# A fixed table of operations and engines in place of a planner, with the shared port handed over both ways

## The chip, the cores and the metric

One core of a Trainium2 chip runs the whole program. It has five engines with a queue each: TensorE (PE) for products, VectorE (DVE), ScalarE (ACT) and GpSimd (POOL) for elementwise work, and SyncE (SP), which here only issues transfers; GpSimd and ScalarE issue transfers too. An instruction waits at the head of its queue for semaphores of other engines, and whatever stands behind it waits with it. The metric is the device time of one execution in microseconds (us), the median of three runs.

## The reference

Attention with a sigmoid in place of the softmax (8 batches, 12 heads, 448 positions of 64 columns), and on its result `x` (8 x 448 x 768) a block with a gate, which is a causal convolution of five taps:

```python
scores = scale * np.matmul(q, k.transpose(0, 1, 3, 2)) - np.log(S)
attn = 1.0 / (1.0 + np.exp(-scores))
x = np.matmul(attn, v)                        # then (B, S, H * D)
for k in range(K):                            # K = 5, xp is x after 4 rows of zeros
    gate_pre += conv_w[k][None, None, :] * xp[:, k:k + S, :]
gate = 1.0 / (1.0 + np.exp(-gate_pre))
val = x @ w_val
return (gate * val @ w_out).astype(np.float32)
```

## The kernel before

**Tiles and stages.** The 96 pairs of batch and head are taken two by two (a pair of heads is 128 partitions), and two such pairs make a "two": 24 of them, three to a batch. For each two PE computes scores (L736, and L780 for the rest of 448 = 3 x 128 + 64), ACT takes the sigmoid (L803) out of the PSUM ring `ps_a` (three buffers), and PE multiplies by `v` (L861, L853). The first nine twos keep the sigmoid in one float32 tile `a_single`. From two 9 on, ACT scales it to an f16 part of `a` (L545 through `scaled`), and DVE makes the remainder (L814); `v` is split likewise into `v_hi` and `v_lo` (L834), and the `qk` of the later pairs into `qk_hi` (a transfer by GpSimd, L711) and `qk_lo` (GpSimd, L550).

The result of a two is copied out of PSUM as `x` (a plain copy for the first twos). Its gate starts with tap 0 as a scaled copy (`gate<-x,cw`); DVE adds taps 1 and 2 (L934), GpSimd makes taps 3 and 4 (`tap`, L931) and adds them by a transfer that accumulates (`gate<-tap`, L938); ACT takes the sigmoid (L940). `x` is split into `xs`, PE makes the val product (L1008), DVE multiplies by the gate (`y`, L1040 and its siblings), `y` is split into `g` and PE makes the out product, for the last three batches in another form (L1100) with `f`, `forms` and `parts`, the last of these added up by L1112 and L1117.

In the first 130 us the weights are made ready besides, six column groups of `w_val` and six of `w_out`: 64-bit words to float32 (`w_words`, of which one step, `rebias`, is a scaled copy), the column's largest value (`val_max`, `out_max`), and a split into `w_val_hi` or `w_out_hi` (`w_hi`) and the remainder (L633).

**What sets the order.** Every operation is recorded with the engines that can do it (`ways`, with a cost in us), a priority and the buffers that it reads and writes. `Plan.issue` then plays the program through as a simulation with those costs: at every time at which an engine is free it takes the ready operation of the least priority. Nearly every priority is overwritten by the tuple `ORDER`, which has one number for each operation. Some scaled copies can go to ACT or DVE (`way`); the simulation sends these to ACT unless ACT is taken for long, but those listed in `ON_VECTOR` go to DVE.

**The shared port.** DVE and GpSimd are taken to share a port, and the simulation lets only one of them run an operation marked `VG` at a time. In the program this becomes a wait in one direction: a GpSimd operation waits for the last DVE operation issued before it. GpSimd's transfers have an empty mark and stand outside of it.

Of the kernel before, what the change touches and what calls it, by code (L numbers as in the profile page):

```python
# [43 lines left out]

# [23 lines left out]

# [3 lines left out]

# [34 lines left out]
AT = dict(  # L107
    first=-4.84, step=186.61, val=-515.91, val_step=75.14, out=-1381.77, out_step=211.97, w_max=499.11,
    w_split=-1182.64, load_qk_first=93.79, load_qk=-2337.48, load_v=1519.38, split_hi=399.85, split_lo=-1153.45,
    rest_first=3068.94, rest=-748.49, a_first=-6991.19, a=-90.43, attend=3226.15, v_max=-214.11, v_exp=-1741.71,  # L110
    v_split=-21.46, x=-2502.94, x_max=-489.67, x_scale=476.16, x_hi=572.53, x_lo=137.58, x_step=3687.57,
    x_early=1650.13, first_max=-343.88, tap=856.2, scores=10.18, a_rest=-547.44, a_rest_first=3711.59,
    tap_first=-337.56, tap_pair=-756.79, tap_step=-337.16, gate=2964.81, product=-1112.59, y=2073.03, g_hi=-1655.49,
    g_lo=-4238.48, o=-5658.32, sums=-1096.57, f=-1122.62, late=-18.26, late_step=570.16, late_load=-455.78,
    pair0=2247.51, pair1=-2185.81, pair2=1410.89, pair3=-3009.11, pair4=1393.75, pair5=-5139.43, pair6=1171.29,
    pair7=-1574.89, pair8=1873.65, pair9=-3931.76, pair10=-780.12, pair11=-656.47, pair12=-3903.55, pair13=-1833.8,
    pair14=1272.88, pair15=-560.26, pair16=527.11, pair17=-4581.08, pair18=-2091.41, pair19=954.34, pair20=113.09,
    pair21=-5387.69, pair22=-2231.28, pair23=643.85, val0=-743.06, val1=1226.04, val2=-946.96, val3=1007.5,
    val4=-4230.95, val5=285.08, out0=79.95, out1=2694.58, out2=3666.47, out3=583.13, out4=2673.53, out5=78.95,
    val_of1=-1932.29, val_of2=-2571.71, val_of3=458.2, val_of4=1531.79, val_of5=1383.92, val_of6=-402.85,  # L120
    val_of7=1447.91, out_of1=621.51, out_of2=-1106.68, out_of3=-2449.73, out_of4=-3262.98, out_of5=101.95,
    out_of6=-338.25, out_of7=-4452.36, share=2435.36, w_load=2254.8,
)
# [1213 lines left out]
```

## Time and profile before

| | us |
|---|---|
| median of 3 runs (lowest to highest) | 573.35 (573.22 to 573.49) |
| span of the profiled execution | 572.0 |
| PE busy | 563.5 |
| DVE busy | 422.3 |
| ACT busy | 403.0 |
| POOL busy | 243.8 |

The span goes from the first to the last recorded instruction of one execution; the median is the device time of other executions of the same program and has 1.35 us around that span. Busy times are for the engine's instructions without semaphore and transfer-issuing ones. A sum for the change is made in the span.

### The profile page before, as it was taken

Reading aid. Unit: us, or ns where it says so; the run is one execution under the profiler, and the core shown is the slowest. Engines: PE = TensorE matmul, PEld = TensorE weight load, DVE = VectorE, ACT = ScalarE, POOL = GpSimd, SP = SyncE. Lnnn points to the kernel's source line nnn. Section 1 sums busy time; section 2 is a strip of 40 time slices with the busy share of each in tenths; the row PEclk is TensorE's granted clock in tenths of the full one; section 3 lists DMA queues with packets and bytes.
Section 4 is the critical chain, followed back from the end, with each engine's and each line's share of the span. In section 5 each row is a group of like instructions: output and inputs, shape, how many; then the busy total and the mean of one; then the engine's idle time right before and its main releaser. Section 6 shows DMA issues by size and latency. Waiting matters only on the chain.

```text
span 572.0 us, 9979 instructions
## 1 busy us (share of the span) xinstructions
PE 563.5 (99%) x3793; PEld 300.7 (53%) x3793; DVE 422.3 (74%) x651; ACT 403.0 (70%) x489; POOL 243.8 (43%) x303
## 2 busy tenths in 40 slices
PE   8999999999999999999999999999999999999996
PEld 4343334354554555545454555455555446865785
DVE  0768899897689784586756788867788999847543
ACT  5788986465987869676686977997889995332221
POOL 0001356755755475356734465544656432500000
PEclk9999999999999999999999999999999999999999
DMA  8878789977677979687395885877778465730122
GB/s 311 342 240 287 226 210 242 212 166 204 205 200 194 326 157 256 158 193 163 92 232 140 213 188 148 218 194 195 192 222 216 141 167 145 188 92 17 58 75 75
DMA packets 48400, 107.25 MB, mean 188 GB/s; under 512 B 15712, under 2 KB 24544, under 8 KB 48352
## 3 DMA queue, kind: packets, MB, share of 16 engines
q1 hardware_dynamic: 33808, 67.19, 34.8%
q0 software_dynamic: 14256, 39.23, 33.4%
q8 instruction: 30, 0.49, 0.3%
q10 hardware_dynamic: 288, 0.20, 0.1%
q14 instruction: 18, 0.15, 0.1%
HBM read 63.52 MB, written 17.90 MB: 142 GB/s over the span
## 4 chain that ended last, share of the span: by engine, by line
PE 95%; ACT 2%; DMA 1%; issue 0%; DVE 0%; SPq 0%; DVEq 0%; ACTq 0%
PE ps_m L1008 45%; PE ps_a L736 16%; PE ps_a L861 16%; PE late L1100 7%; PE ps_a L780 4%; PE ps_m L1100 4%; PE ps_a L853 3%; ACT a_single L803 1%; DMA qk_single<-qk 1%; ACT gate L545 0%; DVE parts L1117 0%; ACT w_words L545 0%; ACT w_val_hi L545 0%; ACT x L539 0%; ACT w_out_hi L545 0%
## 5 line engine op out<-in xcount | busy, mean ns | idle before, releaser
L1008 PE MATMUL ps_m<-xs,w_val_hi 128*128 128x512 f16 x504 | 150.1, 379 | 0.0
L814 DVE SCALAR_TENSOR_TENSOR a<-ps_a,a 128x896 f16<-128x896 f32 x90 | 95.0, 1084 | 27.2 <-ACT a L545 27.1
L803 ACT ACTIVATE ps_a<-ps_a 128x896 f32<-128x896 f32 x105 | 93.1, 912 | 24.8 <-DVE v_exp L793 14.7
L1008 PE MATMUL ps_m<-xs,w_val_lo 128*128 128x512 f16 x252 | 95.5, 379 | 0.0
L550 POOL TENSOR_TENSOR qk_lo<-qk_src,qk_hi 128x448 fp32r<-128x448 f32 x66 | 75.5, 1165 | 40.5 <-DVE gate L934 12.1
L931 POOL TENSOR_SCALAR tap<-x,cw 128x512 f32<-128x512 f32 x84 | 67.5, 832 | 57.3 <-DVE gate L934 12.7
L1008 PE MATMUL ps_m<-g,w_out_hi 128*128 128x512 f16 x288 | 85.8, 380 | 0.0
L545 ACT ACTIVATE a<-ps_a 128x896 f16<-128x896 f32 x90 | 79.9, 930 | 0.1
L1008 PEld LDWEIGHTS <-w_val_hi 128*128 128x128 f16 x504 | 47.6, 98 | 58.3 <-issue 6.8
L934 DVE SCALAR_TENSOR_TENSOR gate<-x,cw,gate 128x512 f32<-128x512 f32 x84 | 66.8, 811 | 0.0
L803 ACT ACTIVATE a_single<-ps_a 128x896 f32<-128x896 f32 x63 | 53.5, 927 | 17.1 <-PE ps_a L736 6.3
L938 POOL DMA_DIRECT2D gate<-tap x42 | 38.5, 917 | 42.3 <-DMA gate<-tap 19.7
L1008 PE MATMUL ps_m<-g,w_out_lo 128*128 128x512 f16 x144 | 54.6, 379 | 0.0
L861 PE MATMUL ps_a<-a,v_hi 128*64 128x448 f16 x360 | 49.4, 355 | 0.0
L1008 PEld LDWEIGHTS <-w_out_hi 128*128 128x128 f16 x288 | 27.0, 98 | 35.0 <-issue 4.3
L861 PE MATMUL ps_a<-a_single,v_src 128*64 128x448 f32 x216 | 42.6, 543 | 0.0
L1008 PEld LDWEIGHTS <-w_val_lo 128*128 128x128 f16 x252 | 24.7, 98 | 29.8
L711 POOL DMA_DIRECT2D qk_hi<-qk x33 | 20.5, 622 | 46.1 <-PE ps_a L736 32.1
L736 PE MATMUL ps_a<-qk_hi 64*128 64x448 f32 x198 | 40.1, 401 | 0.0
L736 PE MATMUL ps_a<-qk_single 64*128 64x448 f32 x180 | 38.1, 558 | 0.7 <-DMA qk_single<-qk 0.5
L736 PE MATMUL ps_a<-qk_lo,qk_hi 64*128 64x448 f32 x198 | 36.4, 363 | 0.0
L736 PE MATMUL ps_a<-qk_hi,qk_lo 64*128 64x448 f32 x198 | 36.3, 362 | 0.0
(144 smaller groups left out, 935.4 us busy)
## 6 DMA issues: line engine op xcount, KB each, us to landing
gate<-tap POOLq DMA_DIRECT2D x42, 512.0 KB, 5.8
qk_src<-qk SPq DMA_DIRECT2D x33, 448.0 KB, 4.7
qk_hi<-qk POOLq DMA_DIRECT2D x33, 416.0 KB, 4.4
v_src<-vs SPq DMA_DIRECT2D x24, 448.0 KB, 4.3
qk_single<-qk SPq DMA_DIRECT2D x14, 448.0 KB, 6.4
out_t<-y SPq DMA_DIRECT2D x24, 224.0 KB, 2.0
w_words<-w_val SPq DMA_DIRECT2D x6, 768.0 KB, 7.9
w_words<-w_out SPq DMA_DIRECT2D x6, 768.0 KB, 5.7
```

Source lines behind the costliest of these rows:

```text
L545: nc.scalar.activation(to, x, AF.Copy, scale=by)
L550: engines[eng].tensor_tensor(to, x, y, op=ALU.subtract)
L736: mm(b()[:, h, :S], k()[rows, at : at + P], q()[rows, :S], start=(n == 0), stop=(n == len(terms(i)) - 1))
L780: mm(b()[to, h, :S], x[n]()[rows, CW:], x[n]()[rows, :S], start=True, stop=True)
L803: nc.scalar.activation(to, b()[:, :, :S], AF.Sigmoid, bias=-math.log(S), scale=1.0 / math.sqrt(D))
L814: op({"V": 1.0}, t + 0.5, lambda e: nc.vector.scalar_tensor_tensor(part(1), p(), A_SCALE, part(0), op0=ALU.mult, op1=ALU.subtract), [b], [ ...
L861: mm(px()[to, p, :S], v()[:, o : o + D], x(st[2 * j + p]["a", c])[:, h, at : at + S], start=(j == 0 and c == 0 and n == 0), stop=(j > 0 an ...
L931: op({"G": TAP_G}, at + AT["tap_step"] * k - AT["tap_first"] + AT["tap_pair"] * p, lambda e, p=p, k=k, tap=tap: nc.gpsimd.tensor_scalar(by ...
L934: op({"V": 0.67}, at + AT["tap_step"] * k + AT["tap_pair"] * p, lambda e, p=p, part=part, k=k: nc.vector.scalar_tensor_tensor(part(), x()[ ...
L938: op({"G": 1.1}, at + AT["tap_step"] * k, lambda e, tap=tap: nc.gpsimd.dma_start(g(), tap(), accum_op=ALU.add), [tap], [g], 4 * P * T * 4, "")
L1008: mm(po()[:, cs], w()[:, c, :], x(k)[:, cs], start=(c == 0 and j == 0), stop=(c == NC - 1 and j == 2))
L1100: mm(po()[:, i * HT : (i + 1) * HT], weights(w, k, c), gv[b, c][g]()[:, x, :], start=(c == 0 and i == 0 and j == 0), stop=(c == UNITS - 1 ...
```

## The change

The operations and what they compute stay. `ORDER` becomes a list of 2436 entries, each an engine's letter and an operation's number, in the order in which they are issued; `Plan.issue` places them so, with no simulation. The costs, the priorities, `AT`, `ON_VECTOR` and `way` go. The waits for the port go both ways between the operations whose key is in `SHARED`: whenever the port goes from one of the two engines to the other, the first operation there waits for the last one here.

```diff
-ON_VECTOR = {
-    "a": {5, 9, 13, 14},
...
+SHARED = {
+    "low", "sign", "rebias", "join", "cw_join", "w_hi", "w_sub", "w_lo", "whole", "w_sums", "form_hi", "form_lo", "y_scale",
+    "o_base", "o_scale", "v_hi", "v_lo", "qk_lo", "edge", "gate", "tap", "tap_g", "xs_hi", "xs_lo", "g_lo", "f", "f_hi",
+    "f_lo", "add",
 }
...
     def issue(self):
...
+        done, placed = set(), []
+        for e, n in ORDER:
+            o = self.ops[n]
+            assert e in o.ways and n not in done, (n, e, o.key)
+            assert all(d.n in done for d in (*o.deps, *(o.after or ()))), (n, o.key)
+            done.add(n)
+            placed.append((e, o))
...
-    for o, p in zip(plan.ops, ORDER):
-        o.prio = p
...
-    for o in plan.issue():
-        o.emit(o.eng)
-        if o.eng in "VG" and o.eng in o.port:
-            traced = nc.cur_bb.bb.instructions[-1]
-            if o.eng == "G" and last is not None:
-                tc.add_manual_dep(traced, last.name, after_vector, reason="port")
-            elif o.eng == "V":
-                last = traced
+    for eng, o in plan.issue():
+        o.emit(eng)
+        if eng in "VG" and o.key[0] in SHARED:
+            last[eng] = traced = nc.cur_bb.bb.instructions[-1]
+            other = last.pop("G" if eng == "V" else "V", None)
+            if other is not None:
+                tc.add_manual_dep(traced, other.name, in_turn, reason="port")
```

`SHARED` leaves out the operations that read PSUM, like `a`, and GpSimd's transfers (`qk_hi`, `gate<-tap`, `g`). Counted over the program, DVE comes to wait at 78 such handovers and GpSimd at 79; before, GpSimd waited for 91 different DVE operations.

Of the 2436 operations 117 change their engine. In the stretches of the trace of before in which they stood:

| stretch, us | ACT to DVE | DVE to GpSimd | GpSimd to DVE |
|---|---|---|---|
| 0 to 83 | 6 `rebias` (one of them of 30 columns), 5 `w_hi`, 3 `gate`, 2 `x` | 1 `w_sub` | |
| 83 to 200 | 3 `a`, 2 `gate`, 2 `v_hi`, 2 `o`, 1 `xs`, 1 `rebias` | 4 `w_sums`, 2 `g`, 1 `whole` | 2 `form`, 1 `whole` |
| 200 to 320 | 10 `a`, 4 `o`, 3 `gate`, 2 `v_hi`, 1 `xs` | | 5 `g` |
| 320 to 480 | 5 `a`, 3 `gate`, 3 `v_hi`, 1 `o`, 1 `xs`, 1 `f` | 3 `g`, 2 `f` | 2 `f`, 1 `g` |
| after 480 | 7 `parts`, 3 `f` | 13 additions of parts, 5 `f` | 2 `f` |

Two of the last stores go from SP to ACT besides. PE's products are the same and in nearly the same order.

The order shows the change at three places. First ACT's queue in the head, around 70 to 83 us of the trace. In these rows `a_single` is the sigmoid, `diagonal` is the scale of `x` for a product of one column; before, it reads:

```order
L803 ACTIVATE a_single<-ps_a 128x896
L545 ACTIVATE w_words<-w_words 128x768 x2
L539 COPY x<-ps_a 128x2x7x64
L803 ACTIVATE a_single<-ps_a 128x896 x3
L545 ACTIVATE gate<-x,cw 128x512
L545 ACTIVATE diagonal<-eye,x_exp 128x128
L545 ACTIVATE gate<-x,cw 128x512
L545 ACTIVATE w_out_hi_93<-w_words,out_scale 128x768
L803 ACTIVATE a_single<-ps_a 128x896 x3
```

and after the change, where the copy of `x` is that of two 4 (above it is that of two 5):

```order
L668 ACTIVATE a_single<-ps_a 128x896
L419 COPY x<-ps_a 128x2x7x64
L668 ACTIVATE a_single<-ps_a 128x896 x6
L425 ACTIVATE w_words<-w_words 128x768 x2
L668 ACTIVATE a_single<-ps_a 128x896 x4
L425 ACTIVATE diagonal<-eye,x_exp 128x128
L668 ACTIVATE a_single<-ps_a 128x896 x3
```

The two `gate` taps, `w_out_hi` and the copy of `x` of two 5 are gone from among the sigmoids.

The copy of `x` of two 5 stands now in DVE's queue, behind the making of weights (the names in brackets are the semaphores that a row waits for; DMAHW is a transfer's):

```order
L490 TENSOR_SCALAR val_inverse<-val_inverse 128x1
L440 TENSOR_SCALAR w_words<-w_words 128x768 [waits DVE_49]
L650 TENSOR_SCALAR first_top<-ps_a 128x3 [waits PE_49]
L652 TENSOR_SCALAR first_top<-first_top 128x1 [waits DVE_49]
L654 TENSOR_SCALAR first_top<-first_top 128x1 [waits DVE_49]
L490 TENSOR_SCALAR val_inverse<-val_inverse 128x1
L462 SCALAR_TENSOR_TENSOR w_words<-w_words 128x768 [waits Activation_49]
L465 TENSOR_REDUCE out_max<-w_words 128x1 [waits DVE_49]
L421 COPY x<-ps_a 128x2x7x64 [waits DMAHW7_49,PE_49]
L777 TENSOR_REDUCE x_max<-x 128x2 [waits DMAHW5_49,DVE_49]
```

Before, DVE had no copy of `x` out of PSUM (`ps_a`) there.

The third place is the queues of DVE and GpSimd around two 19. Before, ACT made `v_hi`, and DVE's `v_lo` waited for ACT alone:

```order
L916 COPY x<-x 128x2x6x4 [waits Activation_49,Pool_49]
L814 SCALAR_TENSOR_TENSOR a<-ps_a,a 128x2x448 [waits PE_49,Activation_49] x2
L834 SCALAR_TENSOR_TENSOR v_lo<-v_src,v_exp,v_hi 128x896 [waits Activation_49]
L814 SCALAR_TENSOR_TENSOR a<-ps_a,a 128x2x448 [waits PE_49,Activation_49] x3
L768 TENSOR_REDUCE vm<-v_src 128x1 [waits DMAHW1_49]
L934 SCALAR_TENSOR_TENSOR gate<-x,cw,gate 128x512 [waits DMAHW3_49,DVE_49,Pool_49]
```

After, DVE makes `v_hi` itself and waits for GpSimd (Pool) ahead of it; the scaled copy of `a` has moved to DVE too:

```order
L633 TENSOR_REDUCE vm<-v_src 128x1 [waits DMAHW7_49]
L427 TENSOR_SCALAR v_hi<-v_src,v_exp 128x896 [waits DVE_49,Pool_49]
L699 SCALAR_TENSOR_TENSOR v_lo<-v_src,v_exp,v_hi 128x896 [waits DVE_49]
L427 TENSOR_SCALAR a<-ps_a 128x2x448 [waits PE_49,Activation_49]
L679 SCALAR_TENSOR_TENSOR a<-ps_a,a 128x2x448 [waits DVE_49]
L679 SCALAR_TENSOR_TENSOR a<-ps_a,a 128x2x448 [waits PE_49,Activation_49]
```

GpSimd's queue there after the change; the last `tap` is the operation that DVE's `v_hi` waits for, and the `gate<-tap` three rows above it waits for an earlier transfer (DMASW):

```order
L795 TENSOR_SCALAR tap<-x,cw 128x512 [waits DMASW4_49]
L795 TENSOR_SCALAR tap<-x,cw 128x512 [waits DMAHW4_49,DMASW2_49,DVE_49]
L795 TENSOR_SCALAR tap<-x,cw 128x512
L577 DMA qk_hi<-qk 128x832 [waits PE_49,Pool_49]
L802 DMA gate<-tap 128x1024 [waits DMASW5_49,DVE_49,Pool_49]
L430 TENSOR_TENSOR qk_lo<-qk_src,qk_hi 128x448 [waits DMAHW5_49,DMASW3_49]
L430 TENSOR_TENSOR qk_lo<-qk_src,qk_hi 128x384
L795 TENSOR_SCALAR tap<-x,cw 128x512
L802 DMA gate<-tap 128x1024 [waits Pool_49]
```

So `v_hi` stands behind whatever holds that transfer's issue.

## Rows read from the trace of the kernel before

**Rows 1.** The page: its first line and busy time by engine.

```profile
span 572.0 us, 9979 instructions
...
PE 563.5 (99%) x3793; PEld 300.7 (53%) x3793; DVE 422.3 (74%) x651; ACT 403.0 (70%) x489; POOL 243.8 (43%) x303
```

**Rows 2.** Busy us by engine, by stretch; then granted clock, DMA share, GB/s.

```profile
17.00:51.00 34.00, 33.83 (x200) 13.04 (x196) 26.26 (x44) 29.69 (x36) 0.51 (x3) 1.00 0.82 282
51.00:83.00 32.00, 30.32 (x179) 11.51 (x177) 28.72 (x59) 28.41 (x37) 11.94 (x13) 1.00 0.79 222
83.00:320.00 237.00, 237.00 (x1519) 118.76 (x1516) 176.96 (x262) 173.11 (x208) 135.79 (x163) 1.00 0.76 199
320.00:480.00 160.00, 160.00 (x1127) 83.24 (x1125) 132.48 (x190) 139.12 (x169) 81.73 (x102) 1.00 0.71 185
480.00:572.00 92.00, 87.00 (x684) 66.63 (x681) 55.49 (x94) 24.48 (x32) 12.91 (x12) 1.00 0.33 90
```

**Rows 3.** Chain of work that ended last, head: start, length in us, what.

```profile
35.40 4.66 PE ps_a L861 x24
...
46.55 4.66 PE ps_a L861 x24
...
58.27 1.26 PE ps_a L861 x5
...
69.81 4.66 PE ps_a L861 x24
...
79.58 0.89 ACT w_out_hi L545
...
83.11 4.66 PE ps_a L861 x24
```

**Rows 4.** PE in order of time, 67 to 83 us; idle before, releaser in brackets.

```profile
67.98 0.16 PE L777 MATMUL ps_a<-first_max,ones 128*128 128x3 bf16 x1 [0.35 <-ACT a_single L803]
...
76.86 0.25 PE L606 MATMUL ps_m<-out_max,ones 128*128 128x1 bf16 x4
...
79.02 0.22 PE L957 MATMUL ps_a<-diagonal,ones 128*128 128x64 bf16 x2 [0.20 <-ACT diagonal L545]
...
81.32 0.59 PE L780 MATMUL ps_a<-qk_single 64*64 64x448 f32 x2 [1.14 <-ACT a_single L803]
```

**Rows 5.** All engines in order of time, the end of the span.

```profile
566.73 0.27 PE L1100 MATMUL late<-forms,w_out_lo 128*128 128x256 f16 x1
566.87 1.14 DVE L1112 SCALAR_TENSOR_TENSOR parts<-late,o_scale,parts 128x512 f32<-128x512 f32 x2
567.64 1.45 SPq L1145 DMA_DIRECT2D out_t<-parts  x3
567.65 0.91 ACTq L1145 DMA_DIRECT2D out_t<-parts  x2
```

**Rows 6.** Durations: ns min/median/max by tile; last two, by line, mean ns.

```profile
L568 DVE TENSOR_SCALAR w_words<-w_words x12: 549/566/623, 13.8 to 116.6; 128x768 int32<-128x768 uint32 x12
...
L633 DVE SCALAR_TENSOR_TENSOR w_out_lo<-w_words,out_scale,w_out_hi x6: 1004/1014/1368, 80.5 to 132.2; 128x768 f16<-128x768 f32 x6
...
L934 DVE SCALAR_TENSOR_TENSOR gate<-x,cw,gate x84: 728/744/1576, 62.3 to 487.5; 128x512 f32<-128x512 f32 x84
...
L938 POOL DMA_DIRECT2D gate<-tap x42: 832/890/1669, 68.5 to 498.2; - x42
...
L931 POOL TENSOR_SCALAR tap<-x,cw x84: 684/694/2971, 53.8 to 493.7; 128x512 f32<-128x512 f32 x84
...
L1117 DVE TENSOR_TENSOR parts<-parts 128x256 f32<-128x256 f32 x27 | 11.6, 428 | 18.0 <-ACT parts L545 18.0
...
L1067 POOL TENSOR_TENSOR f<-y,f 128x256 f32<-128x256 f32 x5 | 3.9, 783 | 24.2 <-ACT forms L539 22.9 <-DVE f L1067 1.2
```

**Rows 7.** Waits: engine, line <- what ended it: us, times, longest.

```profile
POOL gate L938 <- DMA gate<-tap: 19.7, 7, 4.7
...
DVE y L1040 <- POOL tap L931: 2.4, 2, 1.3
```

More of the change, by code (lines that the diff above doesn't have):

```diff
@@ L25 @@
 KT = 5
-TAP_G = 0.65
 P = 128
@@ L104 @@
 ADDED = 2
[L107 to L123, printed above, removed]
@@ L257 @@
+""".split()]
 class Buf:
@@ L293, with __init__, op @@
 class Op:
-    __slots__ = ("ways", "prio", "emit", "deps", "n", "start", "end", "eng", "after", "size", "port", "then")
-    def __init__(self, n, ways, prio, emit, size, port):
-        self.n, self.ways, self.prio, self.emit, self.size, self.port = n, ways, round(prio, 5), emit, size, port
+    __slots__ = ("n", "key", "ways", "emit", "deps", "after", "then", "size")
+    def __init__(self, n, key, ways, emit, size):
+        self.n, self.key, self.ways, self.emit, self.size = n, key, ways, emit, size
         self.deps, self.after, self.then = set(), None, None
-        self.start = self.end = self.eng = None
 class Plan:
-    HOP = {"P": 0.2, "A": 0.13, "V": 0.13, "G": 0.15, "S": 0.0}
-    YIELD = 0.3
-    DMA_RATE = 310e3
-    DMA_DELAY = 2.4
     def __init__(self):
         self.ops = []
-    def op(self, ways, prio, emit, reads=(), writes=(), size=0, port="VG"):
-        o = Op(len(self.ops), ways, prio, emit, size, port)
+    def op(self, key, ways, emit, reads=(), writes=(), size=0):
+        o = Op(len(self.ops), key, ways, emit, size)
         self.ops.append(o)
@@ L348, in issue @@
     def issue(self):
-        waits = [0] * len(self.ops)
-        nexts = [[] for _ in self.ops]
-        follow = [[] for _ in self.ops]
-        for o in self.ops:
-            for d in o.deps:
-                nexts[d.n].append(o)
-            for d in o.after or ():
-                follow[d.n].append(o)
-            waits[o.n] = len(o.deps) + len(o.after or ())
-        engines = "PAVGS"
-        free = dict.fromkeys(engines, 0.0)
-        ready = {e: [] for e in engines}
-        held = dict.fromkeys(engines)
@@ L497, in attention_then_gate @@
     op = plan.op
-    def way(kind, n, scalar, vector):
-        return {"V": vector} if n in ON_VECTOR.get(kind, ()) else {"A": scalar, "V": vector}
     def fixed(shape, dtype, name):
@@ L832, in v_scale @@
         sc = lambda: col(2).bitcast(F32)
-        op(way("v", j, 0.95, 0.6), t + 1, lambda eng: scaled(eng, h(), x(), sc()), [x, e], [h])
-        op({"V": 1.08}, t + 2, lambda _: nc.vector.scalar_tensor_tensor(
+        op(("v_hi", j), "AV", lambda eng: scaled(eng, h(), x(), sc()), [x, e], [h])
+        op(("v_lo", j), "V", lambda _: nc.vector.scalar_tensor_tensor(
             l(), x(), sc(), h(), op0=ALU.mult, op1=ALU.subtract), [x, e, h], [l])
     def attend(j):
-        s, t = two[j], tau(2 * j + 2) + AT["attend"] + shift("attend", j)
+        s = two[j]
         px, single = ps_a.new(), j in WHOLE
@@ L880, in after @@
     def after(j):
-        s, t = two[j], tau(2 * j + 2)
+        s = two[j]
         px, f, c = s["px"], j // 3, j % 3
@@ L924, in after @@
         for p, part in enumerate(parts):
-            op(way("gate", 2 * j + p, 0.61, 0.41), at + AT["tap_pair"] * p, lambda e, p=p, part=part: scaled(
+            op(("gate", j, p), "AV", lambda e, p=p, part=part: scaled(
                 e, part(), x()[:, p, :, HALO:], w(p, 0)), [x, own, cw], [g])
@@ L993, in product, with columns @@
     def product(n, b, m):
-        t = tau((b + 1) * NP) + AT["product"] + (m + NC * (n == "out")) * STEP / 2 + AT.get(f"{n}_of{b}", 0.0) + shift(f"{n}{b}", m)
         h, l = w_hi[n, m], w_lo[n, m]
-        def columns(cs, t):
+        def columns(cs):
             po = ps_m.new()
@@ L1009, in emit @@
                            stop=(c == NC - 1 and j == 2))
-                op({"P": 0.65 * (cs.stop - cs.start) / T}, t + c * STEP / 12, emit, [*reads, h, l], [po])
+                op(("prod", n, b, m, c), "P", emit, [*reads, h, l], [po])
             return po
-        po = columns(slice(0, T), t)
-        t += STEP / 2
+        po = columns(slice(0, T))
         if n == "val":
@@ L1103, in segment @@
                 ws = [q["out", 2 * u + i] for q in (w_hi, w_lo) for i in range(2)]
-                op({"P": 0.33 * len(products)}, t + c * STEP / 40, emit, [*gv[b, c][2], form[u], *ws], [po])
+                op(("late", b, u, n, c, len(products)), "P", emit, [*gv[b, c][2], form[u], *ws], [po])
             return po
-        def copied(n, to, buf, po, t):
-            op(way("parts", 6 * LATE.index(b) + 2 * u + n, 0.64, 0.63), t, lambda e: scaled(
-                e, to(), po()[:, : 2 * HT].rearrange("p (n s) -> p n s", n=2), by()), [po, scale], [buf], port="")
@@ L1116, in add @@
-        def add(t, to, x, z, k, reads, buf):
-            op({"V": 0.07 + 0.00104 * k, "G": 0.1 + 0.0021 * k}, t, lambda e: engines[e].tensor_tensor(
+               [po, scale, *reads], [buf])
+        def add(at, to, x, z, k, reads, buf):
+            op(("add", b, u, at, k), "VG", lambda e: engines[e].tensor_tensor(
                 to(), x(), z(), op=ALU.add), reads, [buf])
-        d, e = STEP / 7, AT["o"] + STEP / 7
         part = lambda n: parts()[:, n]
-        copied(0, lambda: parts()[:, :2], x1, segment(0, t), t + e)
@@ L1130, in late_product @@
+        add(3, lambda: o()[:, 2], lambda: o()[:, 2], lambda: part(1), HT, [x1], c22)
+        added(2, cross, lambda: parts()[:, 2:], [y1], crossed, segment(2))
+        added(1, lambda: o()[:, 1:2], lambda: parts()[:, :1], [x1], c11, segment(3))
         n = (b - 1) * SL
@@ L1143, in late_product @@
         for k, (reads, to, what, size) in enumerate(stores):
-            last = (b, u) == (B - 1, UNITS - 1) and k % 2
-            op({"A": 0.1} if last else {"S": 0.45}, t + STEP + 0.1 * k, lambda e, to=to, what=what: (nc.scalar if e == "A" else nc.sync).dma_start(
+            op(("store", b, u, k), "AS" if (b, u) == (B - 1, UNITS - 1) else "S", lambda e, to=to, what=what: (nc.scalar if e == "A" else nc.sync).dma_start(
                 to(), what()), reads, [], P * 4 * size)
```

515 lines of the change are left out of this document (278 added, 237 removed), and 127 rows, old and new, of the table ORDER.

## The prediction

> **What bounds the kernel now.** I read the page first: TensorE (PE) is busy for 563.5 of the span's 572.0 us, VectorE (DVE) for 422.3, ScalarE (ACT) for 403.0 and GpSimd (POOL) for 243.8 [rows 1]. A change that leaves PE's work alone, as this one does, can only win what PE loses to waits, so the next question is where. The table by stretches answers it [rows 2]: from 83 to 480 us PE is busy for 237.00 of 237 and 160.00 of 160 us, at the full granted clock. It is short in the head (33.83 of 34 and 30.32 of 32 us) and at the end (87.00 of 92).
>
> In the chain of work that ended last the head repeats itself: each two's whole attend products (L861) start one step after those of the two before. An ordinary step is 46.55 − 35.40 = 11.15 us. The next three are 58.27 − 46.55 = 11.72, 69.81 − 58.27 = 11.54 and 83.11 − 69.81 = 13.30 [rows 3], so 0.57 + 0.39 + 2.15 = 3.11 us more than three ordinary ones. The last of them runs through ACT's queue: there `w_out_hi` stands ahead of the `a_single` that PE waits for. PE's own rows name the losses [rows 4]: 0.35, 0.20 and 1.14 us, all released by ACT, together 1.69. The one-column products in these rows (0.16, 0.25 and 0.22, together 0.63) are work that stays. So at most 3.11 − 0.63 = 2.5 us can be had, and 1.69 of it has a name: ACT is late, being busy for 28.41 of 32 us there [rows 2].
>
> At the end the last product is done at 567.00, DVE's last two additions follow, and five stores of the last batch close the span [rows 5], 5.0 us that no product fills.
>
> **The change part by part.** The operations and their data are the same; what changes is who does what, in which order, and the waits between DVE and GpSimd.
>
> *Head: 15 operations of any size leave ACT for DVE* (five `rebias` and five `w_hi` of 128x768, three `gate` taps of 128x512, two copies of `x` of 128x896). At the 0.89 us of the `w_out_hi` piece [rows 3] that is 15×0.89 = 13 us of ACT's time, far more than the 1.69 that PE lost there, so ACT's lateness should go. What they cost on DVE no row shows. Below: DVE's only plain scalar operation of that width takes 0.566 us for 768 columns [rows 6], which in proportion is 0.38 for 512 and 0.66 for 896: 10×0.566 + 3×0.38 + 2×0.66 = 8.1 us. Above: the two-operand forms take 1.014 (768) and 0.744 (512) (both [rows 6]), and 1.014 in proportion for 896 is 1.18: 10.1 + 2.2 + 2.4 = 14.7 us. DVE has 34 − 26.26 + 32 − 28.72 = 11.0 us free there [rows 2], and one `w_sub`, a two-operand form like the 1.014 us row, moves off it: 12.0. The ends lie on both sides of that. I take the lower half, since the moved operations have one tensor operand each, like the 0.566 us row; then DVE holds, with little over. Gain: the 1.69 that is named and a quarter of the 0.8 that isn't, 1.9 us, with bounds of 0 (DVE as late as ACT was) and 2.5.
>
> The place where it would fail is the copy of `x` of two 5, which stands on DVE now behind two steps of `w_words`, `out_max` and five small ones; the PSUM buffer that it empties is one that PE's next scores need.
>
> *Middle, 83 to 480 us.* 45 operations go from ACT to DVE, 12 from DVE to GpSimd and 11 back. PE is covered wherever it is busy for 100% of a stretch: gain nothing, and the cost is nothing too, as long as no ring runs dry. The cover is DVE's slack: 237 − 176.96 = 60 us up to 320, and 160 − 132.48 = 27.5 from 320 to 480 [rows 2]. In the second stretch the moves add 6 to 12 us: ten scaled copies of 896 or 1024 columns at 0.66 to 1.18, three taps and an `o` at 0.38 to 0.74, against five operations that go to GpSimd and three that come back, a net of about −2. DVE then stands at (132.48 + 9) / 160 = 88%, with 18.5 us free.
>
> *Waits both ways.* Before, GpSimd waited for DVE alone. Now DVE waits for GpSimd too wherever GpSimd had the port last: 81 of DVE's rows name it, against 28. What this buys: DVE's `gate` taps take 0.744 us in the median and 1.576 at worst, GpSimd's `tap` 0.694 and 2.971 [rows 6]; that is time of engines off the path, worth nothing to PE after 83 us. What it costs: a wait of DVE on GpSimd's whole queue ahead of it. Behind the waiting `v_hi` of two 19, say, stand `v_lo` and the `a` rows that empty PSUM; PE's next scores need the buffers that those free. A plain handover, with nothing late, is bounded below by nothing and above by the 0.20 us that PE idled before the product behind `diagonal` [rows 4], the shortest wait for another engine in these rows: 79 × 0.20 = 16 us at most, of 18.5 + 60 of slack. I take nothing.
>
> Here a rule of the Trainium skill speaks against the change. The row first: GpSimd's issue of a transfer (`gate<-tap`) takes 0.890 us in the median and 1.669 at worst [rows 6], 0.8 more where something held it. The Trainium skill, page "SBUF — State Buffer", section "Who interferes with whom", says that copies, casts and scalar operations on VectorE can take a port pair that it shares with GpSimd for the whole instruction, GpSimd's descriptor writing included; its section "A bandwidth-pool intuition that's wrong (but worth ruling out)" gives 620 ns for such a transfer alone and 3100 ns beside a VectorE copy. The moved operations are of that kind, and the table's waits leave out GpSimd's issues. By the row, the 60 operations moved from ACT to DVE before 480 us, if each met an issue, would cost GpSimd at most 60×0.8 = 48 us of its 572.0 − 243.8 = 328 us of idle time, hidden. By the page's difference of 2.5 us, an estimate, it would be 150 us, and some of it would show.
>
> *Tail.* The last batch's additions of parts go partly to GpSimd, where a 128x256 addition takes 0.783 us against DVE's 0.428 [rows 6]; DVE so starts its last two about 0.4 earlier. The last five stores go from SP and ACT in parallel (three and two) to four on ACT and one on SP; each takes about 0.45 us to issue [rows 5], so ACT's four take 1.8 where SP's three took 1.45. Sum: +0.1 us, bounds −0.3 and +0.4.
>
> **Sum.** 572.0 − 1.9 + 0 + 0.1 = 570.2 us of span. Around the span of before lie 573.35 − 572.0 = 1.35 us (median less profiled span); with them 571.55, forecast 571.5 us, 0.3% faster. A measurement of this kernel can't tell less than about 0.2% (1.15 us) from no change.
>
> **The rivals.**
> *A: the forecast*, 569.8 to 572.2 us. For it: the 1.14 us behind `w_out_hi` and the ACT releasers [rows 4]. Chance 0.55.
>
> *B: DVE becomes late in the head.* If the moved operations cost the upper 14.7 us, DVE needs 2.7 us more than its 12.0 free, the copy of `x` comes that much late, and PE waits there in place of its wait for ACT: 571.5 + 2.7 = 574.2 us, and 573.4 if 1.9 of it shows. For it: DVE busy for 28.72 of 32 us already. Against: the 0.566 us row. It decides from a price of 0.85 us for a 128x768 scaled copy upward (10×0.85 + 1.7 + 1.8 = 12.0). Chance 0.20, between 572.2 and 574.5.
>
> *C: the handover stalls DVE behind a transfer* (the other side). In the middle GpSimd's queue holds issues of `gate<-tap` that wait for an earlier landing: 7 waits, 19.7 us, 4.7 at the longest [rows 7]. DVE didn't wait for that before. Now an operation such as `v_hi` stands behind the tap behind such an issue, so a DVE queue with PSUM reads behind it takes over the wait. At 19.7 / 7 = 2.8 us each, two that get through to PE cost 5.6: 571.5 + 5.6 = 577.1 us, range 574.5 to 582. It decides where a wait exceeds DVE's slack between handovers, about 18.5 us over some 25 handovers (a third of 78) from 320 to 480, or 0.7 us. For it: that slack is below 2.8. Against: most waits of DVE are for an operation that isn't behind such an issue, and the three PSUM buffers of `ps_a` let PE run ahead by one. Chance 0.18.
>
> *D: GpSimd's issues starve*. As a mechanism of this kernel: the taps come late to `gate`, ACT's sigmoid and DVE's `y` wait, and PE's out products after them. Before, DVE's `y` waited for a tap only twice, 2.4 us in all [rows 7]; as much again in the path is 571.5 + 2.4 = 573.9 us. Chance 0.04. By the page named above this would be the case that decides; the trace's 1.669 so far bears it out only in part.
>
> *E: nothing is gained because the head's end is set by a load* (the change does not do what it says). A step in the head that waited for ACT may wait for `v_src` next, since its load moves behind others in SP's queue: 573.4 us, inside the same bounds as B. Chance 0.03.
>
> **How the numbers follow.** Faster by over 0.2% (below 572.2): A, 0.55. Within 0.2% (572.2 to 574.5): B, D and E, 0.27, less a little that goes beyond: 0.25. Slower: C and that rest, 0.20. The range must leave out no more than 0.2: from A's lower end, 569.8, up to 576.0, which takes in B, D, E and the lower part of C. The likeliest case alone is 569.8 to 572.2.
>
> **What would show it.** In the profile after: the steps of L861 in the head at 11.2 to 11.6 with the last at about 11.7 instead of 13.30; the two products after `diagonal` without a wait for `a_single`; ACT busy in 51 to 83 us well under 28.4 and DVE near 32. PE 100% busy from 83 to 480, and POOL waits with no new DVE row above some 5 us. The worst of the taps near 0.75 on both engines. It is wrong if PE shows waits between 83 and 480 with a DVE releaser (C), if PE's waits in the head are released by DVE's `x` (B), or if scaled copies on DVE take 0.85 us or more.

## The result and the profile after

The changed kernel takes 577.38 us (577.01 to 578.22, 4 runs), the kernel before 573.42 us beside it (573.22 to 574.07, 4 runs): a ratio of 1.0067, 95% interval 1.0055 to 1.0079. It is slower by 0.7% where 0.3% faster was forecast. Its profiled execution has a span of 575.8 us against 572.0 [rows 1].

The page's first line and its busy time by engine:

```profile
span 575.8 us, 9970 instructions
...
PE 565.1 (98%) x3793; PEld 301.1 (52%) x3793; DVE 447.9 (78%) x704; ACT 354.0 (61%) x418; POOL 244.7 (42%) x321
```

PE is busy for 1.6 us longer with the same products, and idle for 575.8 − 565.1 = 10.7 us where it was 572.0 − 563.5 = 8.5: 1.6 + 2.2 = 3.8 us, all of the difference. ACT has 49 us less to do [rows 1] and DVE 26 more. The table by stretches says where (us of the stretch, then busy time of PE, PEld, DVE, ACT and POOL; after them the granted clock):

```profile
17.00:51.00 34.00, 34.00 (x203) 13.64 (x201) 26.34 (x49) 23.73 (x28) 1.68 (x2) 1.00 0.82 273
51.00:83.00 32.00, 32.00 (x194) 12.57 (x192) 28.28 (x53) 24.90 (x31) 9.62 (x14) 1.00 0.72 219
83.00:200.00 117.00, 113.77 (x684) 54.99 (x681) 93.48 (x157) 70.74 (x85) 58.69 (x74) 0.99 0.72 186
200.00:320.00 120.00, 119.43 (x804) 61.28 (x803) 98.72 (x144) 75.12 (x89) 59.00 (x79) 1.00 0.72 188
320.00:480.00 160.00, 159.88 (x1126) 82.78 (x1124) 139.01 (x203) 130.28 (x155) 88.78 (x114) 1.00 0.78 199
480.00:576.00 96.00, 90.11 (x698) 67.91 (x696) 55.88 (x93) 20.91 (x26) 26.07 (x29) 1.00 0.34 95
```

Against [rows 2] the head is now full: 34.00 of 34 and 32.00 of 32, 1.85 us won. From 83 to 480 us, where PE had not missed anything, it misses 3.23 + 0.57 + 0.12 = 3.92 us. At the end, the last product is done at 569.83 + 0.27 = 570.10, so 5.7 us are left behind it instead of 5.0 [rows 5]. The rest of the idle time's account, 2.2 − (3.92 + 0.7 − 1.85) = −0.6, lies before 17 us. There PE waited for a load of `qk_single` in the profile of the kernel before and not in this one:

```profile
7.37 2.53 PE L736 MATMUL ps_a<-qk_single 64*128 64x448 f32 x12 [0.54 <-DMA qk_single<-qk]
```

That is chance and no effect of the change: among the runs below, the one of the planner's kernel with waits both ways lacks this wait, and one of the new table (that with only the 33 marked waits) has it, 0.48 us. So about 0.5 us of the difference between the two spans is hidden by luck.

The step of the head that took 13.30 us, from one two's whole attend products (L726 here) to the next, takes 79.45 − 67.66 = 11.79 now:

```profile
67.66 4.73 PE L726 MATMUL ps_a<-a_single,v_src 128*64 128x448 f32 x24
...
79.45 4.73 PE L726 MATMUL ps_a<-a_single,v_src 128*64 128x448 f32 x24
```

Nearly all of the 3.23 us lie in one place. These are rows of DVE, GpSimd and PE between 100 and 132 us, in order of time by engine (start, length, what; in brackets the idle time before and who ended it):

```profile
107.95 1.40 DVE L900 SCALAR_TENSOR_TENSOR y<-ps_m,y_scale,gate 128x512 f32<-128x512 f32 x2
114.25 0.56 DVE L438 TENSOR_SCALAR w_words<-w_words 128x768 int32<-128x768 uint32 x1 [4.90 <-POOL tap L795]
...
120.92 0.77 DVE L900 SCALAR_TENSOR_TENSOR y<-ps_m,y_scale,gate 128x512 f32<-128x512 f32 x1
...
101.15 0.89 POOL L802 DMA_DIRECT2D gate<-tap  x1 [2.89 <-DVE gate L798]
...
111.87 0.90 POOL L802 DMA_DIRECT2D gate<-tap  x1 [6.49 <-DMA gate<-tap]
...
112.55 1.66 POOL L795 TENSOR_SCALAR tap<-x,cw 128x512 f32<-128x512 f32 x2
...
121.74 0.59 PE L869 MATMUL ps_m<-g,w_out_hi 128*128 128x512 f16 x2 [1.00 <-DVE y L900]
...
130.02 0.38 PE L869 MATMUL ps_m<-g,w_out_hi 128*128 128x512 f16 x1 [1.83 <-DMA g<-y]
130.75 0.38 PE L869 MATMUL ps_m<-g,w_out_hi 128*128 128x512 f16 x1 [0.35 <-DVE g L430]
...
131.64 0.63 PE L869 MATMUL ps_m<-g,w_out_lo 128*128 128x512 f16 x1
```

GpSimd issued a `gate<-tap` at 101.15. Its next one has to wait for that one's landing and sits at the head of the queue, 6.49 us idle, until 111.87. Behind it stand a small fill and two taps (112.55). DVE is done with two `y` at 107.95 + 1.40 = 109.35 and comes to the first step of `w_words` for the fifth column group of `w_out` (L438), whose handover names the second of those taps: 4.90 us idle, until 114.25. The step of `w_words` shares no data with the tap. The `y` at 120.92 stands behind eight more of DVE's rows; PE has waited 1.00 us for it when it starts at 121.74, then 1.83 us for the transfer of a `g` made from a later `y`, and 0.35 us for its remainder: 3.18 us.

Behind these waits products take longer (0.63 us instead of 0.38). The table by stretches for just that time:

```profile
131.60:134.80 3.20, 3.20 (x9) 1.18 (x8) 2.05 (x5) 0.00 (x0) 2.08 (x2) 0.50 0.00 0
```

The granted clock is 0.50, the lower of TensorE's two levels (1.2 GHz of 2.4), for these 3.2 us and for a little of the 0.2 us on either side; from 100 to 131 us and from 135 to 140 it is 1.00. That is where the 1.6 us of added PE time come from: 3.2 us at half clock do the work of 1.6.

### The profile page after: what moved, and what is told of

Same layout as the page of the kernel before. It is cut to its first block, busy times and chain, and to the rows that moved or that the text cites. A ratio compares the mean times of both kernels' runs of the same rounds, so it can differ in the third digit from the quotient of the medians.

```text
span 575.8 us, 9970 instructions
## 1 busy us (share of the span) xinstructions
PE 565.1 (98%) x3793; PEld 301.1 (52%) x3793; DVE 447.9 (78%) x704; ACT 354.0 (61%) x418; POOL 244.7 (42%) x321
## 4 chain that ended last, share of the span: by engine, by line
PE 83%; DMA 6%; DVE 5%; POOL 3%; issue 1%; ACT 0%; POOLq 0%; DVEq 0%
PE ps_m L869 37%; PE ps_a L602 15%; PE ps_a L726 14%; PE late L960 7%; DMA gate<-tap 4%; PE ps_m L960 4%; PE ps_a L645 3%; PE ps_a L718 2%; DMA qk_hi<-qk 1%; DVE gate L798 1%; POOL qk_lo L430 1%; DMA g<-y 1%; POOL tap L795 1%; DVE xs L849 1%; DVE w_words L440 1%
## 5 line engine op out<-in xcount | busy, mean ns | idle before, releaser
L869 PE MATMUL ps_m<-g,w_out_hi 128*128 128x512 f16 x288 | 87.2, 384 | 3.2 <-DMA g<-y 1.8
L795 POOL TENSOR_SCALAR tap<-x,cw 128x512 f32<-128x512 f32 x84 | 60.2, 746 | 67.8 <-issue 14.1
L430 POOL TENSOR_TENSOR qk_lo<-qk_src,qk_hi 128x448 fp32r<-128x448 f32 x66 | 72.7, 1125 | 35.3 <-DVE gate L798 7.3
L425 ACT ACTIVATE a<-ps_a 128x896 f16<-128x896 f32 x75 | 67.6, 917 | 1.6
L798 DVE SCALAR_TENSOR_TENSOR gate<-x,cw,gate 128x512 f32<-128x512 f32 x84 | 59.3, 745 | 3.7 <-POOL tap L795 2.9
L726 PE MATMUL ps_a<-a,v_hi 128*64 128x448 f16 x360 | 49.4, 355 | 0.0
L726 PE MATMUL ps_a<-a_single,v_src 128*64 128x448 f32 x216 | 42.6, 543 | 0.0
```

What stands on the lines that cost most here:

```text
L425: nc.scalar.activation(to, x, AF.Copy, scale=by)
L430: engines[eng].tensor_tensor(to, x, y, op=ALU.subtract)
L726: mm(px()[to, p, :S], v()[:, o : o + D], x(st[2 * j + p]["a", c])[:, h, at : at + S], start=(j == 0 and c == 0 and n == 0), stop=(j > 0 an ...
L795: op(("tap_g", j, p, k), "G", lambda e, p=p, k=k, tap=tap: nc.gpsimd.tensor_scalar(by(tap()[:, p, :]), x()[:, p, :, HALO - k : HALO + SL - ...
L798: op(("tap", j, p, k), "V", lambda e, p=p, part=part, k=k: nc.vector.scalar_tensor_tensor(part(), x()[:, p, :, HALO - k : HALO + SL - k], ...
L869: mm(po()[:, cs], w()[:, c, :], x(k)[:, cs], start=(c == 0 and j == 0), stop=(c == NC - 1 and j == 2))
```

## The experiments

The theory after the result, called theory 1, is the prediction's rival C: VectorE's new waits take over what GpSimd's queue waits for. Theory 2 is that the table itself (its order and DVE's added work) costs; theory 3 that a slow transfer does. All times are medians, each with the kernel before measured on the same chip (573.57, 573.66 and 573.85 us in the three groups); ratios are to it. A difference between runs of two groups is better read from the ratios.

**One wait less.**

```diff
-            if other is not None:
+            if other is not None and o.key != ("low", "out", 4):
                 tc.add_manual_dep(traced, other.name, in_turn, reason="port")
```

> The changed kernel without one single wait: the first step of w_words of the fifth column group of w_out on VectorE (L438, at 114.25 us of the trace after) no longer waits for GpSimd's tap; the other 77 waits of VectorE stay. Theory 1 (this handover is what costs): VectorE starts it at about 109.4 instead of 114.25, the y at 120.92 comes some 4.9 us sooner, PE's waits of 1.00, 1.83 and 0.35 us and the eight products at half clock (1.66 us) go, so 577.4 - 4.8 = 572.6 us, between 572.0 and 573.2. Theory 2 (the table's order and VectorE's added work cost, and the wait only stands where VectorE would be late anyway): 576.5 to 577.5. Theory 3 (the slow landing of 10.17 us of the transfer gate<-tap and the slow g<-y behind it cost): the wait of 1.83 us for g<-y stays, with the clock's fall, 575.5 to 576.5.

Measured: 573.31 us (572.05 to 576.62, 12 runs), ratio 1.0000, interval 0.9985 to 1.0016. One wait out of 78 was worth 577.4 − 573.3 = 4.1 us, somewhat less than the 4.8 expected. Rows of its trace at the same place, GpSimd's queue first, then DVE's:

```profile
112.71 0.90 POOL L802 DMA_DIRECT2D gate<-tap  x1 [6.63 <-DMA gate<-tap]
...
109.97 0.55 DVE L438 TENSOR_SCALAR w_words<-w_words 128x768 int32<-128x768 uint32 x1
...
119.78 0.75 DVE L900 SCALAR_TENSOR_TENSOR y<-ps_m,y_scale,gate 128x512 f32<-128x512 f32 x1 [0.84 <-ACT gate L804]
```

GpSimd's issue still waits for a landing, 6.63 us. But the step of `w_words` (L438) starts at 109.97, straight behind the two `y`, and the late `y` at 119.78; PE's waits of 1.00 and 1.83 us are gone, and its clock from 100 to 140 us is 1.00. Theory 3 is out: the landing is as slow as before and costs PE nothing here once DVE doesn't wait for it. Theory 2 is out as the main cause.

**One way, as before the change.**

```diff
-            if other is not None:
+            if other is not None and eng == "G":
```

> The changed kernel with its table, but the handover one way as before: GpSimd waits for VectorE, VectorE never for GpSimd except for data. Theory 1: all that handovers cost goes, the 4.9 us at 112 to 135 us and a part of the 0.57 us at 218 us: 571.6 to 572.6 us; VectorE's taps and GpSimd's get slow ones again (above 1.5 us at worst), which costs nothing. Theory 2: 576.5 to 577.5.

Measured: 571.79 us (570.80 to 572.62, 5 runs), ratio 0.9965, interval 0.9953 to 0.9976. The whole table with its 117 moved operations is faster than before, by what the prediction had given the change; the second direction alone costs 577.4 − 571.8 = 5.6 us. All of PE's waits in this run (us in total, times, longest):

```profile
PE ps_m L1022 <- DVE ones L1015: 1.1, 1, 1.1
PE ps_m L869 <- DVE g L430: 0.3, 1, 0.3
```

The first is the program's start. GpSimd's taps (ns min/median/max) get their slow ones back, and PE doesn't notice:

```profile
L795 POOL TENSOR_SCALAR tap<-x,cw x84: 681/690/2959, 53.4 to 490.0; 128x512 f32<-128x512 f32 x84
```

**Both ways in the kernel before.** The loop that places the waits, in the planner's kernel:

```diff
-            traced = nc.cur_bb.bb.instructions[-1]
-            if o.eng == "G" and last is not None:
-                tc.add_manual_dep(traced, last.name, after_vector, reason="port")
-            elif o.eng == "V":
-                last = traced
+            turn[o.eng] = traced = nc.cur_bb.bb.instructions[-1]
+            other = turn.pop("G" if o.eng == "V" else "V", None)
+            if other is not None:
+                tc.add_manual_dep(traced, other.name, after_vector, reason="port")
```

> The kernel before, with its planner and its engines, and the handover made both ways as in the changed one. Theory 1 in its broad form (waits of VectorE on GpSimd's queue cost wherever a transfer's issue stands in it): slower than before by 2 us or more, 575.4 or above. Theory 1 in its narrow form (it takes this table's one bad place): 573.0 to 574.5. Theory 2: 573.4, no difference.

Measured: 578.52 us (578.38 to 579.45, 4 runs), ratio 1.0087, interval 1.0074 to 1.0100. The waits cost 5 us there too, with another order and other engines. They are spread here (DVE's longest waits for GpSimd):

```profile
DVE gate L934 <- POOL qk_lo L550: 5.2, 5, 2.2
...
DVE w_words L593 <- POOL tap L931: 2.9, 1, 2.9
```

PE's largest new loss there is to two waits for DVE's `out_max`, 1.4 us together. So the loss isn't the accident of one table.

**Which of the 78 waits.** A first sorting set a mark at an issue of `gate<-tap` by its place in the table and cleared it at DVE's next handover:

```diff
+        behind = behind or o.key[0] == "tap_add"
...
-            if other is not None:
+            if other is not None and (eng == "G" or not behind):
...
+            if other is not None and eng == "V":
+                behind = False
```

> The changed kernel without those of VectorE's 78 handover waits (33) that have an issue of gate<-tap in GpSimd's queue between the operation waited for and the one that VectorE waited for before it; the other 45 stay. Narrow theory (a handover costs where it stands behind a transfer's issue): as fast as one way, 571.4 to 572.4 us. Broad theory (each handover costs, since VectorE takes over GpSimd's whole queue): 573.5 to 576.

and with `behind` in place of `not behind`:

> The complement: only the 33 waits behind an issue of gate<-tap stay, the 45 plain ones go. Narrow theory: all of the loss is here, 576.5 to 578 us. Broad theory: in between, 573.5 to 576.

Measured: 577.36 us (574.13 to 579.36, 8 runs; ratio 1.0058, 1.0038 to 1.0079) without the 33 marked waits, and 571.67 us (570.41 to 573.22, 12 runs; 0.9963, 0.9952 to 0.9974) with those alone. That is the reverse of the narrow theory, and the broad one fails too, since 33 handovers cost nothing. But the sorting didn't do what its expectation says. An issue that stood in the table behind the operation waited for set the mark as well, and the wait at 114.25 us, whose issue had its mark cleared by an earlier handover, was counted as plain. The two runs show that 33 of the waits are free together and that the loss sits in the other 45, no more.

Sorted again, by GpSimd's own queue: the number of its issues is noted with each GpSimd operation that can be waited for, and compared with the number at the last one that DVE waited for.

```diff
+        adds += o.key[0] == "tap_add"
...
+            if eng == "G":
+                at = adds
...
-            if other is not None:
+            if other is not None and (eng == "G" or (at == seen) == True):
...
+            if other is not None and eng == "V":
+                seen = max(seen, at)
```

> The question of the waits that were sorted by place in the table, sorted now by GpSimd's own queue: VectorE keeps the 40 waits for operations ahead of which GpSimd has issued no gate<-tap since the last one that VectorE waited for, and loses the other 38, among them the one at 114.25 us. Narrow theory (a handover costs where a transfer's issue stands ahead of the operation waited for): 571.3 to 572.3 us, as one way. Broad theory (any handover costs): 573 to 576.

and with `False` for the complement:

> The complement: VectorE keeps the 38 waits that stand behind an issue of gate<-tap and loses the 40 plain ones. Narrow theory: 576.5 to 578, as the changed kernel. Broad theory: 573 to 576.

Measured: 573.33 us (571.75 to 575.63, 12 runs; ratio 0.9988, 0.9974 to 1.0002) with the 40 plain waits, 576.25 us (573.20 to 579.47, 12 runs; 1.0042, 1.0024 to 1.0060) with the 38 that stand behind an issue. Above one way that is 573.33 − 571.79 = 1.5 and 576.25 − 571.79 = 4.5 us, together 6.0, about the 5.6 of all 78. By the ratios, since these two were measured beside another run of the kernel before, it is 1.3 and 4.4 of 5.9; the interval of the 40 plain ones just touches that of one way, so their share is barely clear of noise.

These two sums look like a success of the narrow theory, but it does not hold as a rule. Sorted by both rules, 24 of the 38 waits behind an issue are among the 33 that cost nothing. And the run with one wait less, which keeps the other 37, takes 573.31 us, no more than the 573.33 with none of the 38 (by the ratios it is 0.7 us more, within the noise). So nearly all that the 38 cost is the one wait at 114.25 us, which the run that keeps them has again, at 5.8 us. PE waits there for the late `y` (0.75 us) and for the transfer of a `g` once more, but in the profiled execution the clock does not fall (1.00 from 118 to 140 us):

```profile
130.56 0.38 PE L869 MATMUL ps_m<-g,w_out_hi 128*128 128x512 f16 x1 [1.49 <-DMA g<-y]
```

The plain handovers are not free of landings either. The sorting counts issues of `gate<-tap` alone, while GpSimd's `qk_lo` waits for the transfer `qk_hi`. One such chain in the changed kernel, which belongs to the 40:

```profile
211.92 1.13 POOL L430 TENSOR_TENSOR qk_lo<-qk_src,qk_hi 128x448 fp32r<-128x448 f32 x1 [2.21 <-DMA qk_hi<-qk]
...
213.08 0.23 DVE L837 TENSOR_SCALAR o_scale<-o_base,x_exp 128x6 f32<-128x6 f32 x1 [2.69 <-POOL qk_lo L430]
...
218.51 0.47 PE L602 MATMUL ps_a<-qk_hi 64*128 64x448 f32 x2 [0.57 <-DVE v_exp L689]
```

This is the 0.57 us from 200 to 320 us of the table above. In the runs that keep this wait (one wait less, the 40 plain ones) PE loses there too; in those without it (one way, the 38) it is busy for 120.00 of 120.

**No handover at all.**

```diff
-            if other is not None:
+            if other is not None and False:
```

> The table with no handover at all, in neither direction. If the waits of GpSimd for VectorE are worth nothing on the path: 571.4 to 572.2 us, as one way, with VectorE's and GpSimd's slowest taps longer. If they keep VectorE from being held up by GpSimd: slower than one way, 572.5 to 575.

Measured: 592.93 us (590.38 to 597.05, 6 runs), ratio 1.0338, interval 1.0306 to 1.0370. That is 21 us above one way, far beyond both expectations. Busy times (the span is 593.0 us), then the durations of DVE's `gate` taps (ns min/median/max), then rows around 171 us:

```profile
PE 571.8 (96%) x3793; PEld 302.7 (51%) x3793; DVE 497.7 (84%) x704; ACT 354.3 (60%) x418; POOL 257.8 (43%) x321
```

```profile
L798 DVE SCALAR_TENSOR_TENSOR gate<-x,cw,gate x84: 732/744/5583, 61.0 to 514.8; 128x512 f32<-128x512 f32 x84
```

```profile
170.21 7.27 DVE L798 SCALAR_TENSOR_TENSOR gate<-x,cw,gate 128x512 f32<-128x512 f32 x3
...
171.37 0.70 POOL L795 TENSOR_SCALAR tap<-x,cw 128x512 f32<-128x512 f32 x1
...
172.04 1.95 POOL L517 TENSOR_TENSOR w_sums<-w_whole 128x384 f32<-128x384 f32 x2
...
173.95 0.98 POOL L517 TENSOR_TENSOR w_sums<-w_sums,w_whole 128x384 f32<-128x384 f32 x1
...
174.92 1.36 POOL L795 TENSOR_SCALAR tap<-x,cw 128x512 f32<-128x512 f32 x2
```

DVE is busy for 497.7 us instead of the 447.9 with handovers both ways. Its slowest tap takes 5.58 us instead of 0.75: it is one of the three of the first row, and it spans a tap, three `w_sums` and two taps of GpSimd, which follow each other without a gap from 171.37 to 176.28. The wait of GpSimd for DVE, which the kernel before had already, keeps this away: with it alone, one way, the slowest of these taps takes 1.35 us. DVE's waits for GpSimd alone were not run.

**Four operations of the head back on ACT**, on the one-way kernel: in the table `V478` (the copy of `x` of two 5), `V429`, `V430` (two `gate` taps) and `V359` (`w_out_hi`) become `A478`, `A429`, `A430` and `A359`.

> The table with the handover one way, and four operations of the head given back to ScalarE at their places in the table: the copy of x of two 5, two gate taps and the split of the first column group of w_out. Theory of the head (ScalarE's queue held a_single up): the step before two 6 grows from 11.7 to about 13 us again, 571.8 + 1.5 = 573.3 us, 572.8 to 573.6. Rival (the head's gain comes from the loads at its start and the order alone): 571.4 to 572.2.

Measured: 575.01 us (573.27 to 575.71, 12 runs), ratio 1.0018, interval 1.0008 to 1.0028, so 3.2 us above one way and twice what was expected. PE's rows in the step before two 6, with the whole attend products (L726) at which it starts and ends:

```profile
67.81 4.73 PE L726 MATMUL ps_a<-a_single,v_src 128*64 128x448 f32 x24
...
75.22 1.02 PE L602 MATMUL ps_a<-qk_single 64*128 64x448 f32 x4 [0.60 <-ACT a_single L668]
...
79.14 0.22 PE L820 MATMUL ps_a<-diagonal,ones 128*128 128x64 bf16 x2 [0.68 <-ACT diagonal L425]
...
80.82 0.59 PE L645 MATMUL ps_a<-qk_single 64*64 64x448 f32 x2 [0.50 <-ACT a_single L668]
...
82.54 4.73 PE L726 MATMUL ps_a<-a_single,v_src 128*64 128x448 f32 x24
```

The waits for ACT are back: 0.60, 0.68 and 0.50 us, 1.78 together, the last two at the products of [rows 4]. The step takes 82.54 − 67.81 = 14.73 us where it takes 79.88 − 68.10 = 11.78 one way, so 2.95 of the 3.2 us lie in it; the rest of it lies mostly inside PE's rows, where products stand further apart. The head's gain comes from moving these. The step is longer than the 13.30 us of before, so the price of leaving them on ACT in this order is more than what the change gained by them.

**Two stores back on SP**, on the one-way kernel: `A2431` and `A2435` become `S2431` and `S2435`.

> The table with the handover one way, and two of the last five stores issued by SyncE again in place of ScalarE, as before the change. If ScalarE's four issues in a row (1.94 us) set the end: 571.8 - 0.5 = 571.3 us; if the last transfer's landing sets it: 571.8.

Measured: 571.16 us (570.83 to 571.50, 5 runs), ratio 0.9954, interval 0.9940 to 0.9967. That is 0.6 us under one way, but the two intervals overlap by more than half: the difference is not shown. ACT's two issues at the end take 0.98 us, where the four of the changed kernel took 1.94 (its last rows are below), and the tail is no shorter for it. The last product, in a span of 569.3 us:

```profile
563.41 0.27 PE L960 MATMUL late<-forms,w_out_lo 128*128 128x256 f16 x1
```

That leaves 569.3 − 563.68 = 5.6 us behind it, and one way leaves 569.6 − 563.97 = 5.6 as well. So neither branch of the expectation is the answer; what ends the span is told under the tail below. This version beats both kernels; from one way it can't be told apart.

## Why the prediction was wrong, point by point

**The waits both ways, the step that failed.** The prediction priced them at nothing, on an average: 78.5 us of DVE's idle time against 79 handovers of at most 0.20 us. That ceiling was the shortest wait of the rows it was read from, and a wait of PE for ACT. DVE's new waits are longer; beside the one of 4.90 us these are the costliest (us in total, times, longest):

```profile
DVE gate L798 <- POOL tap L795: 2.9, 3, 1.2
DVE o_scale L837 <- POOL qk_lo L430: 2.7, 1, 2.7
```

And a wait isn't paid from a sum over 400 us; it is paid where it falls, and there it was 4.90 us. The prediction's rival C named the mechanism (an operation of DVE behind a tap behind an issue that waits for a landing), its size (2.8 us, 4.7 at the longest [rows 7]) and a point from which it decides (0.7 us of slack for each handover). It was given 0.18 on the argument that most waits aren't behind such an issue. Most aren't (40 of 78), and one that is was enough for some 4 of the 5.6 us. That C's 577.1 us meets the measured 577.4 is luck: C added two mean waits of 2.8 us, and what came was one of 4.90, of which PE lost 3.18, with a fall of the clock behind it. Its point of 0.7 us doesn't sort either: waits like those of 1.2 and 2.7 us above are beyond it, and from 83 to 480 us PE lost no more than 3.92 − 3.18 = 0.74 us to all waits but the one.

The place was wrong as well. It was looked for from 320 to 480 us, since [rows 2] take 83 to 320 as one stretch with 60 us of slack. Cut at 200, DVE is as full in the first part (97.75 of 117 us, 84%) as in the stretch that was looked at (83%):

```profile
83.00:200.00 117.00, 117.00 (x713) 56.97 (x709) 97.75 (x152) 84.06 (x100) 69.55 (x78) 1.00 0.81 220
```

It came at 114 us, where DVE prepares weights, `y` and the first gates in one queue and PE's `ps_m` has two buffers.

**What a late `y` costs.** The prediction counted a wait at its own length. PE lost 3.18 us in this place to its waits, and another 1.6 us to the lower clock after them. The second part is not bound to the first: with the 38 waits kept, PE lost 0.75 + 1.49 + 0.35 us there without a fall of the clock.

**What it buys.** "Worth nothing to PE" is right for the direction added. The taps became even, as forecast (GpSimd's worst is 1.047 us, DVE's 0.752, in the rows below), and with one way they are uneven again at a better time. The prediction didn't ask what the direction that stays is worth; it is 21 us in this table.

**The head.** Right in mechanism and in size. PE's idle time from 17 to 83 us went to zero, 1.85 us for the 1.9 forecast, and the run with four operations back on ACT shows the cause. The 0.5 us before 17 us is chance (see the result). The prices of the moved operations, at the low end of the range or just above (durations in the changed kernel, ns min/median/max, of `rebias`, the split, DVE's tap, GpSimd's issue, GpSimd's tap and the copy of `x`):

```profile
L427 DVE TENSOR_SCALAR w_words<-w_words x6: 552/564/573, 12.6 to 89.2; 128x768 f32<-128x768 f32 x6
...
L427 DVE TENSOR_SCALAR w_out_hi<-w_words,out_scale x1: 611/611/611, 78.8 to 78.8; 128x768 f16<-128x768 f32 x1
...
L798 DVE SCALAR_TENSOR_TENSOR gate<-x,cw,gate x84: 741/746/752, 60.3 to 499.0; 128x512 f32<-128x512 f32 x84
L802 POOL DMA_DIRECT2D gate<-tap x42: 855/893/1330, 66.2 to 531.3; - x42
...
L795 POOL TENSOR_SCALAR tap<-x,cw x84: 681/690/1047, 53.1 to 496.3; 128x512 f32<-128x512 f32 x84
...
L421 DVE COPY x<-ps_a x1: 1091/1091/1091, 72.4 to 72.4; 128x896 f32<-128x896 f32 x1
```

The estimate of 0.566 for a 128x768 scaled copy met 0.564 and 0.611, far below the 0.85 from which rival B decides. The scaled tap 0 took 0.479 in the median for 0.38, and only the copy out of PSUM stands near the upper end, 1.091 for 0.66 to 1.18. B is out: PE waits for nothing from 17 to 83 us, so not for DVE. DVE's 26.34 and 28.28 us there are about those of before although it took on 15 operations, because the table also puts other work of DVE elsewhere (before 17 us it is busy for 6.19 us, where it was 2.40); the prediction's count of DVE's free time left that out. Rival E, a load that sets the head's end, is out with it.

**Rival D.** GpSimd's issues of `gate<-tap` took 0.893 us in the median and 1.330 at worst, against 0.890 and 1.669 [rows 6]. The copies moved to DVE didn't starve them. What the Trainium skill ("SBUF — State Buffer", "Who interferes with whom") says of descriptors held up by VectorE's copies is not borne out by these durations: with more such copies the longest issue is shorter.

**The tail.** It grew by 0.7 us, from 5.0 to 5.7, for the 0.1 forecast, and for a reason that was not in the sum. The rows at the end of the changed kernel:

```profile
569.83 0.27 PE L960 MATMUL late<-forms,w_out_lo 128*128 128x256 f16 x1
...
570.07 1.94 ACTq L1003 DMA_DIRECT2D out_t<-parts  x4
```

and GpSimd's last row, an addition of parts that the change gave it:

```profile
569.26 0.73 POOL L977 TENSOR_TENSOR parts<-parts 128x256 f32<-128x256 f32 x1 [2.49 <-DVE parts L977]
```

The four issues on ACT's queue take 1.94 us, as was worked out (1.8), but they don't set the end. The last store has landed at 573.15, 3.04 us after the last product; before the change it was 3.75. What sets the end is GpSimd. Each engine closes with a drain, an instruction of its queue that the views leave out and the trace records. GpSimd's ends at 574.98, 5.0 us after its last addition, while SP, which waits for the landings, is through at 573.61; 0.8 us of closing instructions follow. Before the change GpSimd's last elementwise row ended at 541.24 and its drain at 546.24, 5.0 us later too and long hidden. In the traces of all ten programs that use the table the end follows GpSimd's drain in this way. So the term that was missing is the drain behind the additions that moved to GpSimd, and putting two stores back on SP could not shorten the tail. No run gives the last addition back to DVE; the 1.4 us between SP's end and GpSimd's are what it could win at most.

**What stays open.** The plain handovers' 1.5 us are explained in part, by the chain behind `qk_lo`. Why some waits of DVE reach PE and others as long don't was not worked out wait by wait. And why the kernels in which DVE keeps waits spread more from run to run (573.20 to 579.47 with the 38, 570.83 to 571.50 in the fastest kernel) was not settled. That a wait behind a landing passes the landing's own scatter on would explain it; no run shows it.

## What to carry to other kernels

A wait that is added for order's sake makes the waiting engine wait for everything ahead of the named instruction in the other queue, transfer issues and their landings included. So look up what stands ahead of it, and price the worst place, not the average over the span. Most such waits cost nothing here, and one cost 4 us: the way to find it is to take single waits out. When two engines share a resource, one direction of waiting can be worth much (21 us here) and the other, added to it, be a loss (5.6 us); try them apart. And before an engine is given work at the very end, look at what its queue does after its last instruction.

## What the runs showed of the hardware

Without handovers a two-operand operation of DVE was held not for one GpSimd instruction but through six that followed each other without a gap (5.58 us where 0.75 is usual). The Trainium skill ("SBUF — State Buffer", "Who interferes with whom") says that a VectorE instruction with two SBUF inputs contends with a GpSimd instruction that reads SBUF, and that whoever issues first gets the shared pair for the whole instruction. The trace agrees that DVE is held up, but here it doesn't get in between two GpSimd instructions, so its price went by the length of GpSimd's run and not of one instruction.

TensorE's granted clock fell to 0.50 after idle stretches of 1.83 and 0.35 us close together, and stayed there for 3.2 us. It stayed at 1.00 around idle stretches of 1.49 and 0.35 us at the same place in the run with the 38 waits, and around one of 1.14 us before the change ([rows 4], [rows 2]).

GpSimd's drain ended 5.0 us after the end of its last elementwise instruction, in the traces of all twelve programs. Where that instruction stood near the end, the drain set the end.
